# 41 matmuls of ones, read by nobody, put into planned TensorE waits of the first batch

## The chip, the cores and the metric

The kernel runs on one core of one Trainium2 chip. The metric is the device time of one execution in microseconds (us). The three runs shown of the kernel before took 528.59, 529.96 and 799.26 us, with a median of 529.96 us. The profile was taken from one further execution, which took 529.17 us.

## The reference

The input is q, k and v of 8 batches, 8 heads, 576 positions and head size 64, and the weights of a gated feed-forward block. What is computed, for each batch:

```python
# attention: heads 0-3 see the last 32 positions, heads 4-7 every 4th of the last 128
scores = where(mask[h], (q @ k.T) / 8, -1e9)           # 576 x 576 per head
attn   = exp(scores - max) / (sum + 1e-9)
x      = (attn @ v)                                    # heads side by side: 576 x 512
# expert
h      = relu(x @ w_in)                                # 576 x 1024
conv   = conv_w[0]*h[s-1] + conv_w[1]*h[s] + conv_w[2]*h[s+1]
out    = (h * sigmoid(conv)) @ w_out                   # 576 x 512
```

## The kernel before

**Tiling.** Attention is done for pairs of heads: four pairs a batch, two with the plain window (kind 0) and two with the dilated one (kind 1), so 32 pairs in all. Scores are computed in strips of 32 queries by 64 keys, since the mask leaves nothing else: one pair is some 72 to 80 small matmuls at line 298 (64x32 weights, 64 columns moving). For the pairs of `EASED`, a few bf16 matmuls of `ones` with the mask (line 285) open the banks first, the maximum is taken straight from PSUM on VectorE (L311 to L315), and nine small exponentials run on ScalarE (L322). VectorE then normalizes and transposes (L340 to L345), and some 84 to 88 small matmuls at line 356 multiply by v. ScalarE copies the result out as the high part (L408, tiles x0a, x1a and so on), and VectorE forms the low part (L411, x0b, x1b), so that products with float32 accuracy can be made from three passes over fp32r operands.

**Expert.** The first product (line 436, 128x288) and the second one (line 478, 128x512) each take three passes per piece (`TERMS`). ScalarE and VectorE do relu, taps, sigmoid and the split of the gated values.

**Weights.** The 16 weight pieces (8 of w_in, 8 of w_out, and one of conv_w) come in as 64-bit floats. For each, ScalarE (L513, L528) and VectorE (L515 to L522) take the words apart, and for ten of them (`SUMMED`) TensorE adds three products in a bank (lines 531 to 533), from which ScalarE copies the low part out (L536). These pieces are prepared in the first batch, among the attention of the first pairs.

**Banks.** PSUM has eight banks of 128x512 float32, all in one tile `banks`. Banks 0 to 3 (pool `att`) are one slot for a pair's scores or its product with v. Banks 4 and 5 (pool `mm`) and 6 and 7 (pool `nn`) serve the expert's products and the sums of the weights; the first pairs in `EARLY` have their scores there.

**Order.** `Planner` holds every piece of work as a task with an engine, a cost in us, a due time and the tasks that it follows. `Planner.order` (line 145) goes through time by these costs: it gives every task a start, picks by due time among the tasks of an engine that could start within 0.25 us of the earliest one, and holds buffers and banks until their last user has ended. The result is one list sorted by planned start, and the instructions are issued in this list's order. Each engine works through its own instructions in that order; what it really waits for on the chip are semaphores, not the planned times. Loads are issued from SyncE's queue (SP) in the same order: qk at L270, v at L272, weights at L504. A load waits there until the tile that it overwrites has been read.

Of the kernel before, what the change touches and what calls it, by code (L numbers as in the profile page):

```python
# [77 lines left out]
EARLY = (0, 1, 3)  # L78
SUMMED = (0, 3, 4, 5, 6, 7, 8, 11, 12, 14)
LEFT = 16  # L80
NU, NX, NR, NW, NT = 10, 7, 4, 3, 2
ONE = dict(start=True, stop=True, skip_group_check=True)

# [17 lines left out]
class Planner:  # L101
# [43 lines left out]
    def order(self):  # L145
        waiting = {t: len(t.after) for t in self.tasks}
        users = {}
        for t in self.tasks:
            for p in t.after:
                users.setdefault(p, []).append(t)  # L150
        ready, last, mode, done = {}, {}, {}, []
        for t in self.tasks:
            if not waiting[t]:
                ready.setdefault(t.engine, []).append(t)
        while len(done) < len(self.tasks):
            best = None
            for e, ts in ready.items():
                at = [(self.start(t, last.get(e), mode.get(e)), t) for t in ts]
                at = [x for x in at if x[0] is not None]
                if not at:  # L160
                    continue
                first = min(x[0] for x in at)
                s, t = min((x for x in at if x[0] <= first + self.WINDOW), key=lambda x: (x[1].due, x[0]))
                if best is None or first < best[0]:
                    best = (first, s, t)
            _, s, t = best
            for b in t.uses:
                if b.t is None:
                    slot = min(self.free[b.pool])
                    self.free[b.pool].remove(slot)  # L170
                    b.t, b.slot = slot[2], slot
            t.end, last[t.engine] = s + t.cost, t
            if t.table is not None:
                mode[t.engine] = t.table
            for b in t.uses:
                b.left -= 1
                b.end = max(b.end, t.end + self.late(t))
                if not b.left:
                    self.free[b.pool].append((b.end, b.slot[1], b.slot[2]))
            ready[t.engine].remove(t)  # L180
            done.append((s, t))
            for n in users.get(t, ()):
                waiting[n] -= 1
                if not waiting[n]:
                    ready.setdefault(n.engine, []).append(n)
        return [t for _, t in sorted(done, key=lambda x: x[0])]


@with_exitstack
def attn_moe(ctx: ExitStack, tc: tile.TileContext, qk_p, qk_d, v_p, v_d, w_in, w_out, conv, mask, out):  # L190
    nc = tc.nc
# [7 lines left out]
    ones = const.tile([128, 128], BF16, name="ones")  # L199
# [3 lines left out]
    plan = Planner()  # L203
# [23 lines left out]
    banks = psum.tile([128, 8, 512], F32, name="banks")  # L227
# [3 lines left out]
    bank = lambda ps: banks[:, ps.t]  # L231
    chunk = lambda u, n=512: u.t[:, LEFT:LEFT + n]
    body = lambda u: u.t[:, 1:S + 1]
# [313 lines left out]
    made = plan.add("POOL", 0.6, -1e4, lambda: make_identity(nc, ident))  # L547
    made = plan.add("ACT", 0.29, -1e4, lambda: nc.scalar.copy(out=ones, in_=ident), [made])
# [21 lines left out]
    wored = [weights(w_out[c], 512, WO[c], pair=(wo[0][c], wo[1][c]), summed=c + NF in SUMMED) for c in range(NF)]  # L570
    for b in range(B):
        expert(b, [attention(b, p) for p in range(NP)], wired, wored, conved)
    with tc.manual_schedule():
        for t in plan.order():
            t.run()


def _layouts(q, k, v, moe_w_in, moe_conv_w, moe_w_out):
# [84 lines left out]
```

## Time and profile before

| what | value |
|---|---|
| profiled execution | 529.17 us |
| its span, first to last instruction | 527.4 us |
| time around the span | 1.77 us |
| TensorE (PE) matmuls | 505.9 us busy, 7656 matmuls |
| PE weight loads (PEld) | 442.2 us busy |
| VectorE (DVE) | 393.4 us |
| ScalarE (ACT) | 304.9 us |
| mean granted TensorE clock | 0.984 |
| share of PE in the chain of waits | 92% |

The page of the profile divides the span in 40 slices and gives the busy share of each engine and the TensorE clock that was granted. The chain of waits goes back from the last instruction to whatever released each step. The timeline lists instructions in order of time; neighbours of one kind are drawn together, and an idle time ahead of a row stands in brackets with what ended it. "issue" is time in which the engine waited for nothing that the profile shows. Ends of matmuls are modelled, so the time from one row's start to the next row's start is the better measure of what a group of matmuls takes.

### The profile page before, as it was taken

What the parts mean: (1) busy time and instruction counts of PE and PEld (TensorE: products, weight loads), DVE (VectorE), ACT (ScalarE), POOL (GpSimd) and SP (SyncE); (2) the same over time, 40 slices, a digit from 0 to 9 for tenths busy, and PEclk for the clock granted to TensorE, in tenths of its full rate; (3) what the DMA queues carried; (4) which work ended last, traced back from release to release, by engine and by line L of the source; (5) the groups of instructions that cost most, each with busy time, mean ns of one, the idle gap of its engine ahead of it and who ended that gap; (6) DMA issues with size and microseconds to landing.
All of it is one profiled execution on the core that took longest, in us unless ns stands there. A gap on an engine that the chain in (4) does not pass through costs nothing.

```text
span 527.4 us, 17134 instructions
## 1 busy us (share of the span) xinstructions
PE 505.9 (96%) x7656; PEld 442.2 (84%) x7656; DVE 393.4 (75%) x675; ACT 304.9 (58%) x642; POOL 1.4 (0%) x26
## 2 busy tenths in 40 slices
PE   4579999999999999999999999999999999999997
PEld 3457988988877899879988889899889988998885
DVE  5877998999999789968989639997789730872400
ACT  5856887746842267626677337766757631852410
POOL 1000000000000000000000000000000000000000
PEclk9868999999999999999999999999999999999999
DMA  8966654001154541151152224320310011101111
GB/s 300 354 214 225 179 186 170 1 0 62 51 170 156 206 136 36 54 162 52 48 163 95 61 73 150 94 85 21 118 40 21 1 22 41 40 2 41 40 41 60
DMA packets 17274, 52.33 MB, mean 99 GB/s; under 512 B 2096, under 2 KB 2480, under 8 KB 17200
## 3 DMA queue, kind: packets, MB, share of 16 engines
q1 hardware_dynamic: 17200, 51.23, 29.3%
q8 instruction: 60, 0.98, 0.8%
q14 instruction: 14, 0.11, 0.1%
HBM read 41.79 MB, written 9.44 MB: 97 GB/s over the span
## 4 chain that ended last, share of the span: by engine, by line
PE 92%; DMA 3%; ACT 2%; issue 1%; DVE 1%; SPq 0%; ACTq 0%
PE banks L436 40%; PE banks L478 38%; PE banks L356 7%; PE banks L298 6%; PE banks L531 2%; ACT s L322 1%; DMA raw<-in_w_out_dram 1%; DMA qk<-in_qk_d_dram 1%; PE banks L533 0%; PE banks L532 0%; PE banks L285 0%; DVE x2b L411 0%; SPq L504 0%; SPq L270 0%; DVE w L517 0%
## 5 line engine op out<-in xcount | busy, mean ns | idle before, releaser
L448 DVE SCALAR_TENSOR_TENSOR u<-u,conv_sb,u 128x576 f32<-128x576 f32 x128 | 103.5, 816 | 12.9 <-ACT u L454 11.4
L443 ACT ACTIVATE u<-banks 128x288 f32<-128x288 f32 x128 | 51.4, 410 | 52.0 <-PE banks L436 50.6
L489 ACT COPY u<-banks 128x512 f32<-128x512 f32 (+1 forms) x37 | 21.1, 572 | 77.3 <-PE banks L478 76.2
L461 DVE TENSOR_TENSOR u<-u,u 128x576 f32<-128x576 f32 x64 | 47.9, 757 | 11.0 <-ACT u L459 9.9
L459 ACT ACTIVATE u<-u 128x576 f32<-128x576 f32 x64 | 42.9, 683 | 18.4 <-DVE u L448 17.8
L454 ACT ACTIVATE u<-u,conv_sb 128x576 f32<-128x576 f32 x64 | 49.8, 779 | 1.6
L356 PEld LDWEIGHTS banks<-pt,v 32*64 32x64 f32 x2752 | 36.4, 137 | 16.7 <-issue 7.3
L356 PE MATMUL banks<-pt,v 32*64 32x64 f32 (+2 forms) x2752 | 40.5, 233 | 7.2 <-ACT s L322 3.9
L436 PE MATMUL banks<-x2a,wi 128*128 128x288 f32 x160 | 46.0, 302 | 0.0
L436 PE MATMUL banks<-x3a,wi 128*128 128x288 f32 x160 | 45.7, 302 | 0.0
L436 PE MATMUL banks<-x0a,wi 128*128 128x288 f32 x160 | 45.4, 301 | 0.0
L436 PE MATMUL banks<-x1a,wi 128*128 128x288 f32 x160 | 45.2, 298 | 0.0
L298 PE MATMUL banks<-qk 64*32 64x64 f32 x2432 | 35.7, 232 | 9.7 <-DMA qk<-in_qk_p_dram 6.9
L436 PE MATMUL banks<-x4a,wi 128*128 128x288 f32 x160 | 45.0, 296 | 0.0
L298 PEld LDWEIGHTS banks<-qk 64*32 64x32 f32 x2432 | 29.8, 109 | 16.7 <-DMA qk<-in_qk_p_dram 6.9
L436 PE MATMUL banks<-x5a,wi 128*128 128x288 f32 x128 | 36.2, 299 | 0.0
L436 PEld LDWEIGHTS banks<-x2a,wi 128*128 128x128 f32 x160 | 30.3, 189 | 1.5 <-ACT u L443 0.5
L436 PEld LDWEIGHTS banks<-x3a,wi 128*128 128x128 f32 x160 | 29.9, 188 | 1.0 <-ACT u L443 0.2
L436 PEld LDWEIGHTS banks<-x0a,wi 128*128 128x128 f32 x160 | 29.9, 188 | 0.8
L436 PEld LDWEIGHTS banks<-x1a,wi 128*128 128x128 f32 x160 | 30.0, 188 | 0.4
L436 PEld LDWEIGHTS banks<-x4a,wi 128*128 128x128 f32 x160 | 30.0, 188 | 0.2
L478 PE MATMUL banks<-wo,g1a 128*128 128x512 f32 x72 | 28.7, 398 | 0.0
(136 smaller groups left out, 1271.8 us busy)
## 6 DMA issues: line engine op xcount, KB each, us to landing
qk<-in_qk_d_dram SPq DMA_DIRECT2D x16, 672.0 KB, 4.6
qk<-in_qk_p_dram SPq DMA_DIRECT2D x16, 592.0 KB, 4.0
out_dram<-u SPq DMA_DIRECT2D x31, 256.0 KB, 2.0
v<-in_v_p_dram SPq DMA_DIRECT2D x16, 384.0 KB, 3.5
v<-in_v_d_dram SPq DMA_DIRECT2D x16, 384.0 KB, 3.7
raw<-in_w_out_dram SPq DMA_DIRECT2D x8, 512.0 KB, 3.7
raw<-in_w_in_dram SPq DMA_DIRECT2D x8, 512.0 KB, 5.1
out_dram<-u SPq DMA_DIRECT2D x10, 128.0 KB, 2.3
```

The lines of the kernel that those rows point to most:

```text
L298: nc.tensor.matmul(banks[quad * 32:quad * 32 + 32, at[bank], c * W:c * W + W], q, k, start=i == 0 and not eased, stop=i == len(parts) - 1, ...
L322: nc.scalar.activation(out=s.t[:, i, :], in_=banks[:, at[bank], c * W:c * W + W], func=AF.Exp, scale=SCALE, bias=m.t[:, i:i + 1], accum_ou ...
L356: nc.tensor.matmul(banks[hd * 64:hd * 64 + 64, bank, o:o + n], v.t[quad * 32:quad * 32 + 32, block // 2, block % 2 * 64:block % 2 * 64 + 6 ...
L436: nc.tensor.matmul(bank(ps)[:, 0:HALF], wi[jw][fc][:, k * 128:k * 128 + 128], x[k].t[jx][:, hf * HALF:hf * HALF + HALF], start=(k == 0 and ...
L443: relu.append(plan.add("ACT", 0.4, due + 1.6 * u + relued, lambda fc=fc, hf=hf, ps=ps: nc.scalar.activation(out=h[fc].t[:, 1 + hf * HALF:1 ...
L448: nc.vector.scalar_tensor_tensor(out=body(c[fc]), in0=h[fc].t[:, k:S + k], scalar=conv_sb[:, k, fc:fc + 1], in1=body(c[fc]), op0=ALU.mult, ...
L454: t = plan.add("ACT", 0.777, d, lambda fc=fc: nc.scalar.activation(out=body(c[fc]), in_=body(h[fc]), func=AF.Copy, scale=conv_sb[:, 1, fc: ...
L459: t = plan.add("ACT", 0.686, d + shaped, lambda fc=fc: nc.scalar.activation(out=body(c[fc]), in_=body(c[fc]), func=AF.Sigmoid), [t], [c[fc ...
L461: t = plan.add("DVE", 0.755, d + times, lambda fc=fc: nc.vector.tensor_tensor(out=body(c[fc]), in0=body(c[fc]), in1=body(h[fc]), op=ALU.mu ...
L478: nc.tensor.matmul(bank(ps), g[k].t[jg][:, col:col + 128], wo[jw][k], start=(k == 0 and i == 0), stop=(k == NF - 1 and i == 2))
L489: t = plan.add("ACT", 0.16 + 0.00093 * (c1 - c0), out_due + by_block * u + copied, lambda ps=ps, o=o, c0=c0, c1=c1: nc.scalar.copy(out=chu ...
L531: nc.tensor.matmul(bank(ps), ident, words(t), start=True, stop=False)
```

## The change

`order` now also keeps each task's planned start (`start_at`) and returns the planned starts with the tasks. A new function `filled` walks through TensorE's tasks up to a planned start of 60 us (`FILLED`). Where the plan has a gap between the end of one task and the start of the next, it looks for a bank of the pools `mm` and `nn` that no task holds over the whole gap, and puts as many fill matmuls there as the gap holds, by 0.43 us each in the first gap and 0.23 us each in the later ones, rounded down. A fill multiplies the 128x128 bf16 tile `ones` with 512 columns made of the same tile, into the free bank. Nothing reads what it writes. The fills stand in TensorE's instruction order just ahead of the task whose planned start ends the gap. Due times, costs and the order of all other tasks are as they were. A fill that writes a bank which another engine has read also waits for that reading to have ended.

Going through the plan's costs gives these 41 fills:

| planned gap (us in the plan) | fills | bank | task that follows | that task's first row in the timeline before |
|---|---|---|---|---|
| 2.84 to 6.90 | 9 | 7 | scores, first pair | 6.91 |
| 7.61 to 8.66 | 4 | 7 | scores, second | 8.21 |
| 10.42 to 10.66 | 1 | 7 | weight sum | 10.62 |
| 16.94 to 17.42 | 2 | 7 | scores, fourth | 16.91 |
| 19.03 to 21.58 | 11 | 6 | product with v, first | 20.95 |
| 22.53 to 24.17 | 7 | 6 | scores, fifth | 23.91 |
| 25.78 to 26.02 | 1 | 7 | weight sum | 27.96 |
| 28.49 to 28.73 | 1 | 7 | weight sum | 32.62 |
| 34.71 to 34.95 | 1 | 7 | weight sum | 39.63 |
| 37.68 to 37.92 | 1 | 7 | first product, L436 | 44.09 |
| 41.27 to 41.51 | 1 | 7 | first product, L436 | 47.34 |
| 47.18 to 47.42 | 1 | 6 | weight sum | 53.17 |
| 52.67 to 52.91 | 1 | 6 | first product, L436 | 58.82 |

The planned gaps ahead of the second and third product with v (30.16 to 31.04 and 31.85 to 33.90, rows 35.48 and 38.58) get none, because every bank of the two pools is held there.

```diff
+FILLED = 60.0
...
-            t.end, last[t.engine] = s + t.cost, t
+            t.start_at, t.end, last[t.engine] = s, s + t.cost, t
...
-        return [t for _, t in sorted(done, key=lambda x: x[0])]
+        return sorted(done, key=lambda x: x[0])
+
+    def filled(self, done, fill, first, until, pools, step):
+
+        held = {}
+        for _, t in done:
+            for b in t.uses:
+                if b.pool in pools:
+                    h = held.setdefault(b, [b.t, t.start_at, t.end])
+                    h[2] = max(h[2], t.end + self.late(t))
+        at, more = first.end + self.late(first), []
+        first = at
+        for s, t in done:
+            if t.engine != "PE" or s > until:
+                continue
+            free = [i for p in pools for _, i in pools[p] if all(h[0] != i or h[2] <= at or h[1] >= s for h in held.values())]
+            for k in range(int((s - at) / step[at == first]) if free else 0):
+                more.append((at + 0.001 * k, lambda i=free[-1]: fill(i)))
+            at = t.end
+        return [run for _, run in sorted([(s, t.run) for s, t in done] + more, key=lambda x: x[0])]
...
+    def fill(i):
+        nc.tensor.matmul(banks[:, i], ones, ones.unsqueeze(1).to_broadcast([128, 4, 128]), start=True, stop=True)
+
+    spots = {p: [(0, i) for i in n] for p, n in (("mm", (4, 5)), ("nn", (6, 7)))}
     with tc.manual_schedule():
-        for t in plan.order():
-            t.run()
+        for run in plan.filled(plan.order(), fill, made, FILLED, spots, (0.23, 0.43)):
+            run()
```

## The prediction

> **What bounds the kernel now.** I read the page first, then the granted clock by stage, then TensorE's timeline, then who releases its waits.
>
> ```profile
> span 527.4 us, 17134 instructions
> PE 505.9 (96%) x7656; PEld 442.2 (84%) x7656; DVE 393.4 (75%) x675; ACT 304.9 (58%) x642; POOL 1.4 (0%) x26
> ```
>
> TensorE is busy in all but 21.5 us of the span, so the bulk of the kernel can't be touched by 41 matmuls. All that can move is in the first 45 us. Busy time by stage, cut where the granted clock changes (columns: stretch and length, PE, PEld, DVE, ACT, POOL, granted clock, DMA share, GB/s):
>
> ```profile
> 16.10:19.50 3.40, 2.14 (x80) 1.33 (x78) 2.57 (x7) 1.03 (x2) 0.00 (x0) 1.00 0.89 324
> 19.50:22.90 3.40, 0.80 (x46) 0.67 (x50) 2.78 (x9) 3.40 (x24) 0.00 (x0) 1.00 1.02 407
> 22.90:26.30 3.40, 2.62 (x118) 2.09 (x114) 3.18 (x7) 3.40 (x19) 0.00 (x0) 0.50 0.95 330
> 26.30:29.70 3.40, 2.42 (x35) 1.12 (x18) 3.31 (x7) 1.03 (x2) 0.00 (x0) 0.50 0.74 250
> 29.70:33.20 3.50, 3.50 (x92) 2.58 (x91) 2.06 (x6) 1.62 (x4) 0.00 (x0) 0.50 0.90 303
> 33.20:36.60 3.40, 3.40 (x82) 1.80 (x83) 2.98 (x8) 2.89 (x19) 0.00 (x0) 0.50 0.42 124
> 36.60:40.00 3.40, 1.74 (x116) 1.51 (x104) 2.20 (x5) 2.54 (x6) 0.00 (x0) 1.00 0.57 204
> 40.00:43.40 3.40, 3.40 (x42) 2.09 (x43) 2.94 (x6) 1.55 (x4) 0.00 (x0) 0.50 0.56 187
> ```
>
> The clock changes in steps of 3.4 us. It fell to half after a step with 0.80 us of TensorE work (19.5 to 22.9), stayed there for four steps, came back at 36.6 after two steps without a pause, fell once more after a step with 1.74 us (36.6 to 40.0), and came back at 43.4. So 17 us ran at half clock. A step with 2.14 us of work (16.1 to 19.5) did not make it fall. TensorE's waits there:
>
> ```profile
> 6.91 1.36 PE L298 MATMUL banks<-qk 64*32 64x64 f32 x72 [6.91 <-DMA qk<-in_qk_p_dram]
> ...
> 17.27 0.97 PE L298 MATMUL banks<-qk 64*32 64x64 f32 x72
> 20.95 0.33 PE L356 MATMUL banks<-pt,v 32*64 32x64 f32 x4 [2.71 <-ACT s L322]
> 22.43 1.55 PE L356 MATMUL banks<-pt,v 32*64 32x64 f32 x84 [1.15 <-ACT s L322]
> ...
> 25.08 0.42 PE L285 MATMUL banks<-kinds_sb,ones 128*128 128x256 bf16 x2 [0.78 <-ACT s L322]
> ...
> 27.55 0.48 PE L298 MATMUL banks<-qk 64*32 64x64 f32 x13 [0.98 <-issue]
> ```
>
> The same 72 score matmuls took 1.36 us at 6.91 and 0.97 at 17.27, so the start of the kernel was slow too. The waits at 20.95, 22.43 and 25.08 are for the exponentials on ScalarE, which reads the banks that TensorE wants. ScalarE in turn waited for a load, as the chain of waits has it (start, us, what):
>
> ```profile
> 11.56 7.47 DMA raw<-in_w_out_dram
> 19.04 0.02 issue
> 19.06 0.66 ACT w L513
> ```
>
> Up to 25.08 the bound is thus the load that lands at 19.03 and ScalarE behind it (3.40 us busy of 3.40 in both stages from 19.5). From 25.08 to 36.9 it is TensorE at half clock.
>
> **What half clock costs.** Sums of weights (E, lines 531 to 533), products with v (V, line 356) and first products (line 436), at half and at full clock, from start to start:
>
> ```profile
> 27.96 2.08 PE L531 MATMUL banks<-w,ident 128*128 128x512 f32 x2
> ...
> 30.82 1.87 PE L356 MATMUL banks<-pt,v 32*64 32x64 f32 x88
> 32.62 2.08 PE L531 MATMUL banks<-w,ident 128*128 128x512 f32 x2
> ...
> 35.48 1.44 PE L356 MATMUL banks<-pt,v 32*64 32x32 f32 x84
> 38.58 1.12 PE L356 MATMUL banks<-pt,v 32*64 32x32 f32 x84 [1.66 <-DVE x2b L411]
> 39.63 1.76 PE L531 MATMUL banks<-w,ident 128*128 128x512 f32 x2
> ...
> 44.09 0.40 PE L436 MATMUL banks<-x2a,wi 128*128 128x288 f32 x1
> ...
> 53.17 1.12 PE L531 MATMUL banks<-w,ident 128*128 128x512 f32 x2
> ...
> 54.60 0.29 PE L436 MATMUL banks<-x1a,wi 128*128 128x288 f32 x1
> ...
> 55.01 0.29 PE L436 MATMUL banks<-x0a,wi 128*128 128x288 f32 x1
> ...
> 57.50 1.40 PE L356 MATMUL banks<-pt,v 32*64 32x64 f32 x88
> 58.82 0.40 PE L436 MATMUL banks<-x2a,wi 128*128 128x288 f32 x1
> ```
>
> An E takes 2.86 us at half clock (27.96 to 30.82, and 32.62 to 35.48) and 1.43 at full (53.17 to 54.60). A V of 88 takes 1.80 against 1.32; one of 84 takes 1.44 (row 35.48) against 1.05 (38.58 to 39.63). The stretch 39.63 to 44.09, an E, three first products and a V of 84, takes 4.46; at full clock 1.43 + 0.41 + 1.05 = 2.89, so 1.57 less.
>
> **The change, part by part.** A fill is nearest to a second product, which also moves 512 columns; at half clock to a pass of an E:
>
> ```profile
> 35.12 0.43 PE banks L533
> ...
> 87.45 0.69 PE banks L478 x3
> ```
>
> So 0.23 us a fill at full clock and 0.43 at half.
>
> *Nine, four, one and two fills (ahead of rows 6.91, 8.21, 10.62, 16.91).* The nine take 3.9 us at half clock and lie in TensorE's 6.91 us of waiting for the first qk; cost nothing. The four take 0.9 to 1.7 us between the first and the second scores, the other three 0.7 to 1.3. They can make these scores late by up to 1.7 us, and with them SP's loads that overwrite qk. I take nothing, because all that follows waits for the load landing at 19.03 with the DMA engines 0.89 to 1.02 busy; without that cover it would be +1.7. On the other side the clock may come up before 9 us, worth 1.36 - 0.97 = 0.4 at each score group, equally hidden.
>
> *Eleven fills (ahead of 20.95).* 11 x 0.23 = 2.5 us inside the 2.71 of idle time. Cost nothing; if they start late, TensorE still has 1.15 us of waiting at 22.43. Their use is the clock: the stage 19.5 to 22.9 goes from 0.80 us of work to about 2.0 (0.80 and what of the fills lies behind 19.5). That is near the 2.14 that held and above the 1.74 that did not. I take it that it holds.
>
> *Seven fills (ahead of 23.91).* With full clock the V at 22.43 ends 22.43 + 1.12 = 23.55, seven fills end at 25.16, and scores, openings included (0.42), start at 25.6 and end at 26.6, or at 27.5 if the 0.98 of issue stays, against 27.96.
>
> *The chain after that.* The next waits come from these rows of DVE and ACT:
>
> ```profile
> 29.16 0.69 DVE L522 SCALAR_TENSOR_TENSOR r<-raw,w 128x512 fp32r<-128x512 uint32 x1
> ...
> 32.10 0.43 DVE L515 TENSOR_SCALAR w<-w 128x512 int32<-128x512 int32 x1 [1.44 <-ACT w L513]
> ...
> 33.46 0.82 DVE L411 TENSOR_TENSOR x1b<-banks,x1a 128x512 fp32r<-128x512 f32 x2 [0.20 <-ACT x1a L408]
> ...
> 37.70 0.82 DVE L411 TENSOR_TENSOR x2b<-banks,x2a 128x320 fp32r<-128x320 f32 x2 [1.16 <-ACT x2a L408]
> ...
> 32.73 0.70 ACT L408 CAST x1a<-banks 128x64 fp32r<-128x64 f32 x2 [0.65 <-PE banks L356]
> ...
> 36.97 0.70 ACT L408 CAST x2a<-banks 128x256 fp32r<-128x256 f32 x2 [0.88 <-PE banks L356]
> ```
>
> First E and V: 26.6 to 27.5, plus 1.43 + 1.32 and two single fills, gives 29.8 to 30.7. The second E needs r, done at 29.85, and ends at 31.3 to 32.2 (before: 35.48). The V behind it needs the bank that x1b reads until 34.28. That moves only by DVE's 1.44 of waiting, which ends with TensorE's first E: to 32.84, so this V gains 35.48 - 32.84 = 2.6. The next V waits for x2a and x2b. On ACT, x2a stands behind nine exponentials, which wait for the same piece of DVE's work and move with its 1.44; x2a had then waited 0.88 more for TensorE, and that goes: 1.44 + 0.88 = 2.3. ACT's 0.65 ahead of x1a can go too, if the first V is early enough for it: 2.9. I take the middle, 2.6. VectorE thus keeps what TensorE alone would have saved beyond it: twice 1.43, 0.48 and 0.39 are 3.7, and the issue wait.
>
> *The stretch from 39.63* gains 1.57 with full clock. The two Vs ahead of it keep waits of over a microsecond between them and get no fills, as now, when the clock fell in that step. Between 0 and 1.57 I take 0.3.
>
> *Seven single fills.* Two are in the sum above. The other five stand where TensorE has no wait (39.63, 44.09, 47.34, 53.17, 58.82) and each delays all behind it: 5 x 0.23 = 1.15; 1.35 if one runs at half clock, 0 if the change of shape there hides it. I take 1.15.
>
> Behind that TensorE no longer waits:
>
> ```profile
> 43.40:46.80 3.40, 3.40 (x135) 2.50 (x126) 1.82 (x4) 1.85 (x4) 0.00 (x0) 1.00 0.41 139
> ```
>
> From here a shift of its work goes to the end, as PE carries the chain. **Sum:** 2.6 + 0.3 - 1.15 = 1.75 us less: 529.17 - 1.75 = 527.4 us. The profiled execution lies 0.8 below the median of the runs shown (529.96); I allow that much either way.
>
> **Rivals.** *The clock stays full throughout* (chance 0.2). For it: idle times after the change are short. Against it: 36.6 to 40.0, where 1.74 us of work were not enough, and no fills come there. The time: 2.9 + 1.57 - 1.15 = 3.3 less, 525.9. [...]
>
> *No gain* (0.15). The clock falls a step later, or VectorE, over 9 tenths busy from 22.9 to 29.7, keeps all but about 1.15 us, which the five single fills use up: 529.2.
>
> *Slower* (0.12): the eleven don't hold the clock, since most of them lie ahead of 19.5 or the steps lie otherwise, and the seven run at half clock in front of the scores. They end at 22.43 + 1.55 + 3.01 = 27.0 instead of 25.08: +1.9, all of it on TensorE's chain up to 36.9. Two single fills at 0.43 and the other five for 1.35 make 4.1: 533.3. It decides at whether the first E still takes 2.86. If the seven bring the clock back by the next step, this rival is gone, since then an E saves 1.43 again.
>
> *Instruction supply.* The issue wait of 0.98 us in the scores at 27.55 shows that TensorE's stream can stop for itself. 41 matmuls and their weight loads shift where such stops fall, all through the kernel. I have no reason for a sign: 1 us either way, in the range and in no chance; 0.03 is left for what I don't see.
>
> **How the numbers follow.** My forecast has 0.5 and lies from 526.4 to 528.4. With the full clock (0.2; its lower end 2.9 + 1.57 - 0.2 = 4.3 less, 524.9) and no gain (0.15; upper end 529.2 + 0.8 and half of the 1 us above) the range is 524.9 to 530.5. A difference of 2%, about what a measurement of this kernel can tell from no change, is 10.6 us. All half-clock time together is worth 17 / 2 = 8.5, less than that, and the slower rival is at 0.8%. Faster by over 2%: 0.01, slower by over 2%: 0.02, within: 0.97.
>
> **What would show it.** Right: granted clock 1.00 from 22.9 on in the changed trace, E from 27 at 1.43 us each, V's wait for x2b longer than 1.66, VectorE's wait of 1.44 for L513 gone, single fills with no wait ahead of them, everything from 45 us on about 1.8 us earlier. The step on the second fall: half clock for one step near 37 to 40. Wrong: an E of 2.86 behind the fills, scores later than 25.44, a fill waiting for ACT, or new issue waits of a microsecond.

## The result, and the profile after

The changed kernel took 524.73 us in the median (523.14 to 526.7) against 529.94 for the kernel before: a ratio of 0.9904 with a 95% interval from 0.9874 to 0.9933. Three later comparisons of the same kernel on other occasions gave 0.993, 0.994 and 0.9926 (below), so the gain is 3.3 to 5.2 us. The forecast was 527.4 with a range from 524.9 to 530.5: right in direction, too small in size. The three later times, 524.98, 525.73 and 525.44 us, lie inside that range; the first lies just below it. Its profiled execution took 524.88 us.

The page of the changed kernel, first lines:

```profile
span 523.1 us, 17214 instructions
PE 509.4 (97%) x7697; PEld 443.1 (85%) x7697; DVE 392.7 (75%) x675; ACT 304.5 (58%) x642; POOL 1.4 (0%) x26
```

Busy time by stage in the changed kernel (columns as in the prediction):

```profile
16.80:20.20 3.40, 3.40 (x88) 1.92 (x86) 2.27 (x7) 2.10 (x11) 0.00 (x0) 1.00 1.01 394
20.20:23.60 3.40, 2.44 (x94) 1.67 (x93) 3.06 (x10) 3.40 (x25) 0.00 (x0) 1.00 1.01 398
23.60:27.00 3.40, 3.40 (x86) 2.10 (x83) 3.15 (x8) 2.41 (x10) 0.00 (x0) 1.00 0.93 311
27.00:30.40 3.40, 2.55 (x94) 1.84 (x92) 3.37 (x9) 2.43 (x6) 0.00 (x0) 1.00 0.65 215
30.40:33.80 3.40, 1.96 (x87) 1.19 (x85) 3.33 (x9) 3.40 (x21) 0.00 (x0) 1.00 0.70 264
33.80:37.20 3.40, 2.66 (x86) 2.11 (x87) 2.76 (x6) 2.11 (x5) 0.00 (x0) 0.51 0.82 282
37.20:40.60 3.40, 3.40 (x56) 2.28 (x55) 2.25 (x5) 1.10 (x2) 0.00 (x0) 0.50 0.35 112
```

The clock stayed full from 16.8 to 33.8 and then fell for two steps of 3.4 us, after a step with 1.96 us of TensorE work. That is one execution: in the three later profiles of the same kernel the clock fell near 16 for one step, and again near 36 to 37 for one or two. TensorE's timeline in the changed kernel (start, length; L596 are the fills, L319 scores, L552 weight sums, L377 products with v, L457 first products):

```profile
17.95 2.55 PE L596 MATMUL banks<-ones 128*128 128x512 bf16 x11
20.43 0.33 PE L377 MATMUL banks<-pt,v 32*64 32x64 f32 x4
...
22.84 1.68 PE L596 MATMUL banks<-ones 128*128 128x512 bf16 x7
...
24.70 1.00 PE L319 MATMUL banks<-qk 64*32 64x64 f32 x72
...
25.86 1.02 PE L552 MATMUL banks<-w,ident 128*128 128x512 f32 x2
...
29.18 0.42 PE L377 MATMUL banks<-pt,v 32*64 32x16 f32 x12 [0.85 <-issue]
...
29.76 1.02 PE L552 MATMUL banks<-w,ident 128*128 128x512 f32 x2
...
31.68 1.11 PE L377 MATMUL banks<-pt,v 32*64 32x32 f32 x84 [0.43 <-DVE x1b L432]
34.54 1.59 PE L377 MATMUL banks<-pt,v 32*64 32x32 f32 x84 [1.75 <-DVE x2b L432]
...
36.47 1.91 PE L552 MATMUL banks<-w,ident 128*128 128x512 f32 x2
...
41.24 0.48 PE L457 MATMUL banks<-x2a,wi 128*128 128x288 f32 x1
...
55.98 0.49 PE L457 MATMUL banks<-x2a,wi 128*128 128x288 f32 x1
```

Set against the rows of before, the first weight sum is 2.10 us earlier (27.96 to 25.86), the third product with v 4.04 (38.58 to 34.54), and the row of 58.82 is 2.84 earlier. The span is 4.3 shorter. So some 1.5 us were won behind 56 us, where the change added nothing. That shows in TensorE's waits behind 62 us, all of kind "issue" (total us, times, longest), first before, with the longest of them as a row of the timeline, then after:

```profile
PE banks L356 <- issue: 1.7, 2, 1.1
PE banks L298 <- issue: 0.8, 1, 0.8
```

```profile
86.52 0.33 PE L356 MATMUL banks<-pt,v 32*64 32x32 f32 x12 [1.11 <-issue]
```

```profile
PE banks L377 <- issue: 1.2, 1, 1.2
```

The three waits before stand in the chain of waits, at 85.42, 184.03 and 236.41 us (1.11, 0.60 and 0.79 us), and so does the one of 1.24 us after, at 81.97.

### The profile page after: what moved, and what is told of

Same layout as the page of the kernel before. It is cut to its first block, busy times and chain, and to the rows that moved or that the text cites. A ratio compares the mean times of both kernels' runs of the same rounds, so it can differ in the third digit from the quotient of the medians.

```text
span 523.1 us, 17214 instructions
## 1 busy us (share of the span) xinstructions
PE 509.4 (97%) x7697; PEld 443.1 (85%) x7697; DVE 392.7 (75%) x675; ACT 304.5 (58%) x642; POOL 1.4 (0%) x26
## 4 chain that ended last, share of the span: by engine, by line
PE 94%; DMA 3%; ACT 1%; issue 1%; SPq 0%; DVE 0%; ACTq 0%
PE banks L457 40%; PE banks L499 38%; PE banks L377 7%; PE banks L319 6%; PE banks L552 1%; DMA raw<-in_w_out_dram 1%; DMA qk<-in_qk_d_dram 1%; ACT s L343 1%; PE banks L596 1%; PE banks L554 0%; PE banks L553 0%; PE banks L306 0%; SPq L293 0%; DVE x2b L432 0%; SPq L525 0%
## 5 line engine op out<-in xcount | busy, mean ns | idle before, releaser
L469 DVE SCALAR_TENSOR_TENSOR u<-u,conv_sb,u 128x576 f32<-128x576 f32 x128 | 103.5, 817 | 12.7 <-ACT u L475 11.1
L377 PEld LDWEIGHTS banks<-pt,v 32*64 32x64 f32 x2752 | 35.6, 134 | 14.4 <-issue 7.8
L457 PE MATMUL banks<-x2a,wi 128*128 128x288 f32 x160 | 46.1, 303 | 0.0
L457 PE MATMUL banks<-x3a,wi 128*128 128x288 f32 x160 | 45.7, 302 | 0.0
L457 PE MATMUL banks<-x0a,wi 128*128 128x288 f32 x160 | 45.4, 300 | 0.0
L457 PE MATMUL banks<-x1a,wi 128*128 128x288 f32 x160 | 45.3, 298 | 0.0
L457 PE MATMUL banks<-x4a,wi 128*128 128x288 f32 x160 | 45.2, 297 | 0.0
L377 PE MATMUL banks<-pt,v 32*64 32x64 f32 (+2 forms) x2752 | 39.7, 230 | 5.2 <-issue 2.1
L319 PEld LDWEIGHTS banks<-qk 64*32 64x32 f32 x2432 | 28.7, 106 | 9.7 <-issue 4.0
L319 PE MATMUL banks<-qk 64*32 64x64 f32 x2432 | 34.2, 224 | 2.3 <-DMA qk<-in_qk_d_dram 2.1
L457 PE MATMUL banks<-x5a,wi 128*128 128x288 f32 x128 | 36.2, 299 | 0.0
L457 PEld LDWEIGHTS banks<-x2a,wi 128*128 128x128 f32 x160 | 30.3, 190 | 1.4 <-ACT u L464 0.5
L457 PEld LDWEIGHTS banks<-x3a,wi 128*128 128x128 f32 x160 | 30.0, 188 | 1.0 <-ACT u L464 0.2
L457 PEld LDWEIGHTS banks<-x0a,wi 128*128 128x128 f32 x160 | 29.9, 188 | 0.8
L457 PEld LDWEIGHTS banks<-x1a,wi 128*128 128x128 f32 x160 | 30.0, 188 | 0.4
L457 PEld LDWEIGHTS banks<-x4a,wi 128*128 128x128 f32 x160 | 30.0, 188 | 0.1
```

The lines of the kernel that those rows point to most:

```text
L319: nc.tensor.matmul(banks[quad * 32:quad * 32 + 32, at[bank], c * W:c * W + W], q, k, start=i == 0 and not eased, stop=i == len(parts) - 1, ...
L377: nc.tensor.matmul(banks[hd * 64:hd * 64 + 64, bank, o:o + n], v.t[quad * 32:quad * 32 + 32, block // 2, block % 2 * 64:block % 2 * 64 + 6 ...
L457: nc.tensor.matmul(bank(ps)[:, 0:HALF], wi[jw][fc][:, k * 128:k * 128 + 128], x[k].t[jx][:, hf * HALF:hf * HALF + HALF], start=(k == 0 and ...
L469: nc.vector.scalar_tensor_tensor(out=body(c[fc]), in0=h[fc].t[:, k:S + k], scalar=conv_sb[:, k, fc:fc + 1], in1=body(c[fc]), op0=ALU.mult, ...
```

## The experiments

Two theories stood against each other. A: the gain is the clock. B: TensorE's instruction stream is loaded in pieces (before, the page has 60 packets on the queue q8, "instruction", for 15,312 matmuls and weight loads, some 255 each); the 82 added instructions (41 matmuls with their weight loads) shift where it is cut, and so where TensorE waits for its own instructions. The times are medians, with the kernel before run beside them on the same chip. The diffs are shortened, and the comments in them were added here.

**Small fills at the same places.** The same 41, with 1 column in place of 512:

```diff
-        nc.tensor.matmul(banks[:, i], ones, ones.unsqueeze(1).to_broadcast([128, 4, 128]), start=True, stop=True)
+        nc.tensor.matmul(banks[:, i, 0:1], ones, ones[:, 0:1], start=True, stop=True)
```

> The same 41 matmuls at the same places, but with 1 column moving in place of 512, so that TensorE's instruction stream is as long as in the changed kernel and the waits stay idle. Theory A (the gain is the clock): half clock comes back as before, some 17 us of it between 20 and 45, the first weight sum (L531 of before, near 27) takes 2.86 us, and the row that stood at 58.82 before stays within 1 us of it; time within 1.5 us of before. Theory B (a good part of the gain is a shifted instruction supply): the issue waits change as in the changed kernel (0.98 in the scores gone, one of 1.2 instead of three for 2.5 us behind 62), and 1.3 to 2.3 us of the 5 us are kept with the clock still falling.

This gave 524.82 us against 528.74, ratio 0.9931 (0.99 to 0.9961): most of the gain is there without TensorE being kept busy. In this kernel's stages the clock fell at 23.2 as before, but came back two steps earlier:

```profile
19.80:23.20 3.40, 1.02 (x71) 0.88 (x72) 2.99 (x9) 3.40 (x26) 0.00 (x0) 1.00 1.01 399
23.20:26.60 3.40, 2.68 (x121) 2.07 (x110) 3.18 (x7) 3.40 (x18) 0.00 (x0) 0.50 0.90 320
26.60:30.00 3.40, 3.40 (x36) 1.55 (x33) 3.33 (x9) 0.80 (x2) 0.00 (x0) 0.50 0.92 324
30.00:33.40 3.40, 3.02 (x124) 2.07 (x126) 2.85 (x7) 3.31 (x15) 0.00 (x0) 0.99 0.75 236
```

Its timeline has no issue wait in the fifth scores, and behind 62 us its issue waits are one of 0.2. The load that landed at 19.03 before landed at 19.12 here, and the third product with v still started 2.46 us earlier than before (36.12 instead of 38.58):

```profile
25.52 1.56 PE L319 MATMUL banks<-qk 64*32 64x64 f32 x72
...
27.06 2.06 PE L552 MATMUL banks<-w,ident 128*128 128x512 f32 x2
...
36.12 1.32 PE L377 MATMUL banks<-pt,v 32*64 32x32 f32 x84 [1.87 <-DVE x2b L432]
```

```profile
PE banks L377 <- issue: 0.2, 1, 0.2
```

**The shift by itself.** Small matmuls only in TensorE's first wait, 41, 64 or 128 of them, and the changed kernel for comparison:

```diff
+        more = [(first + 0.001 * k, lambda: fill(7)) for k in range(41)]      # or 64, 128; no others, 1 column each
```

> The changed kernel itself once more, as the corner of a square of four: fills of 512 columns and 82 instructions more. Both theories: about 0.990 of before. It is there so that the other three are compared with it on the same chip.

> No fills; 41 matmuls of 1 column in TensorE's first wait, ahead of the first scores, where it idles for 4 us: the instruction stream is moved by 82 instructions and nothing else. Theory A (clock): as before, ratio 0.998 to 1.002. Theory B (the instruction stream comes in pieces of 256 instructions, 60 packets of 16 KB for some 15,300 instructions, and where a piece ends decides how long TensorE waits for the next): as the 41 small fills, near 0.993, with the issue wait in the scores at 27 gone and at most 1.2 us of issue waits behind 62 us.

> The same with 128 matmuls of 1 column, so 256 instructions: the pieces end at the same work as in the kernel before. Theory B: the gain of the 41 is gone, ratio 0.998 to 1.002, issue waits again in the scores near 27 and of some 2.5 us behind 62. If it stays near 0.993, it isn't where the pieces end, but something else that the small matmuls bring.

> 64 matmuls of 1 column in the first wait, half a piece of the instruction stream. If where the pieces end is what decides, the issue waits come at the same counts of matmuls from the start as in all other traces (350, 477, 605 and so on, steps of 128), whatever stands there, and so in other places of the work than with 0, 41 or 128; the ratio can lie anywhere from 0.993 to 1.003. If waits come at the same places of the work as in one of those, the pieces are not the cause.

The changed kernel gave a ratio of 0.993 (0.9903 to 0.9957); 41 in front 0.995 (0.9932 to 0.9968); 64 in front 0.9962 (0.9939 to 0.9985); 128 in front 1.0022 (1.0 to 1.0043). With 256 instructions more the gain is gone, and the wait in the fifth scores stands at the same place of the work as before, behind 59 of 72 matmuls (shift of 128):

```profile
26.91 1.13 PE L322 MATMUL banks<-qk 64*32 64x64 f32 x59
28.89 0.47 PE L322 MATMUL banks<-qk 64*32 64x64 f32 x13 [0.85 <-issue]
```

How many matmuls had started when a wait of this kind ended is in the PE column of a stretch from 0 to that time. Before, up to the wait in the fifth scores:

```profile
0.00:27.50 27.50, 14.00 (x477) 9.71 (x478) 19.75 (x49) 18.43 (x75) 1.37 (x26) 0.92 0.90 328
```

With the shift of 128, and with that of 41 (two waits):

```profile
0.00:28.80 28.80, 17.50 (x605) 13.05 (x606) 19.70 (x48) 18.37 (x75) 1.37 (x26) 0.93 0.87 311
```

```profile
0.00:20.00 20.00, 9.95 (x350) 7.32 (x350) 12.63 (x31) 11.12 (x35) 1.37 (x26) 1.00 0.86 301
0.00:31.90 31.90, 18.11 (x605) 12.70 (x605) 23.16 (x56) 20.23 (x78) 1.37 (x26) 0.89 0.89 314
```

In the changed kernel, up to the wait at 29.18:

```profile
0.00:29.10 29.10, 22.87 (x605) 13.33 (x605) 21.94 (x54) 20.01 (x78) 1.37 (x26) 1.00 0.92 342
```

350, 477, 605: steps of 127 or 128 matmuls, with their weight loads some 255 instructions. Where there is such a wait, it stands at one of these counts, whatever work is there. With 64 in front the counts 350 and 477 fall in the fourth scores, behind 32, and one matmul ahead of the end of the first product with v:

```profile
17.66 0.45 PE L322 MATMUL banks<-qk 64*32 64x64 f32 x32
19.84 0.66 PE L322 MATMUL banks<-qk 64*32 64x64 f32 x40 [1.72 <-issue]
...
23.64 1.70 PE L380 MATMUL banks<-pt,v 32*64 32x64 f32 x83 [1.15 <-ACT s L346]
26.60 0.21 PE L380 MATMUL banks<-pt,v 32*64 32x32 f32 x1 [1.26 <-issue]
```

The trace also has the times of the instruction queue's packets (q8 on the page: 60 packets, 0.98 MB, so 16 KB each). Each of these waits ended 1.2 to 1.6 us after one of them:

```
kernel      matmuls before the wait   packet            TensorE goes on   later by
before      477                       25.05 to 26.05    27.55             1.51
before      1751                      84.18 to 85.12    86.52             1.40
before      3281                      182.03 to 183.35  184.63            1.29
before      4173                      235.01 to 235.97  237.20            1.23
after       605                       26.48 to 27.58    29.18             1.60
after       1752                      80.88 to 81.82    83.21             1.38
shift 128   350                       14.44 to 15.33    16.94             1.61
shift 128   605                       26.37 to 27.47    28.89             1.43
shift 128   1879                      83.98 to 84.91    86.37             1.46
shift 128   4301                      236.12 to 237.07  238.39            1.32
```

1751 and 1879, 4173 and 4301 lie 128 apart, as a shift by one piece demands. The steps of some 255 instructions agree with the 15,312 over 60 packets.

The other traces bear this out. In the 20 traces together TensorE's timelines have 80 issue waits of 0.1 us or more. Each stands within 4 matmuls of a count of 222 + 127.45 k, and the packet that ended last ahead of it is in every case packet k of its trace, counted from 0; TensorE went on 1.21 to 1.61 us after its end. The places are thus fixed by the program. The lengths are not: with 41 more matmuls the issue waits behind 62 us come to 0.2 and 0.8 us in the two profiles with small fills, to 0.7 to 1.2 in the four of the changed kernel, and to 1.7 with all 41 in front.

**Full fills at a shift of 128.** The four large gaps in finer pieces, 36, 16, 40 and 26 matmuls of 128 columns:

```diff
+            n = {9: 36, 4: 16, 11: 40, 7: 26}.get(n, n)
+            few = n < 3        # 512 columns as before; the others 128
```

> The fills at their places and about as long as in the changed kernel, but cut into 36, 16, 40 and 26 matmuls of 128 columns in the four large gaps, 128 matmuls in all, so 256 instructions: clock as in the changed kernel, pieces ending as before. Theory A: ratio 0.990. Theory B alone: 1.000. Both add: about 0.996, half clock for 7 us or less, and issue waits of some 2.5 us behind 62.

This gave 529.19 against 528.78, ratio 0.9993 (0.9969 to 1.0017). That is 1.05 us below the 128 small ones (530.24), which is less than these runs can tell from nothing. There was half as much time at half clock (mean granted clock 0.993 against 0.985), and no gain over before: nearest to Theory B alone. The count of 477 falls in the first product with v here, behind 56 of its 88 matmuls, and the wait there was 2.34 us:

```profile
22.28 0.79 PE L380 MATMUL banks<-pt,v 32*64 32x64 f32 x52 [0.16 <-ACT s L346]
25.41 0.58 PE L380 MATMUL banks<-pt,v 32*64 32x32 f32 x32 [2.34 <-issue]
```

**Which fills.** Parts of the change alone (the others left out):

```diff
+            n = n if 19.0 < at < 23.0 else 0      # late18: the eleven and the seven
+            n = n if n > 1 else 0                 # nosingle34: no gap of one fill
```

> Only the eleven and the seven fills (planned gaps 19.03 and 22.53). Theory A: the clock holds from 22.9 to about 34, and the row of 58.82 comes at 55.5 to 56.5: the five single fills (1.15) are gone, and the 0.7 that the changed kernel had won before 20 us may be lost. A rival: without the first sixteen, the start runs at half clock until 12.7 as before, the steps lie otherwise, and the clock falls near 23 all the same: no gain, or a loss of up to 2 us from fills at 0.43.

> Without the eight gaps of one fill each (one ahead of the first weight sum, seven from planned 25.8 on): 9, 4, 2, 11 and 7 are left. If a single fill costs its 0.23, the row of 58.82 comes about 1.2 us earlier than in the changed kernel (55.98), at 54.8, and the time is some 1.2 less than the changed kernel's. If they cost nothing (hidden in the change of shape) it stays at 56.0. If they do hold the clock, half clock lasts longer than the 6.8 us of the changed kernel.

> As nosingle34, and also 6 and 15 fills of 256 columns in the two planned gaps where every bank is held (ahead of the second and third product with v, rows 31.68 and 34.54 of the changed kernel), written without a start flag to the upper half of bank 4, which nobody reads. Theory A: the second fall of the clock (33.9 in the changed kernel) does not come, weight sum and products from 36.5 to 41.2 take 1.5 us less, and the time is 1.5 to 2.5 below nosingle34, about 521.5. Rival: the products with v wait for VectorE and start no earlier, the fills delay them by up to 0.5 us each, and nothing is gained over nosingle34.

*late18*: 526.8 against 528.74, ratio 0.9961 (0.9931 to 0.9991). The clock held from 13.5 to 37.4, so in this execution the front fills weren't needed for that, and the fifth scores had an issue wait of 0.96 again: with 18 ahead, the count of 477 falls in them, behind 41 of their 72 matmuls. *nosingle34*: 524.18, ratio 0.9908 (0.9877 to 0.994). (It has 33 fills, as the single one ahead of the first weight sum went too.) *held* (fills of 256 columns also ahead of the second and third product with v, in columns that nobody reads): 525.45, ratio 0.9937 (0.9914 to 0.9959), against what I expected. Its mean granted clock was the highest of these, 0.996, and its time 4 us above the 521.5 that I had put down; it also has another shift, 54, and its fills hold back the second product with v, as the first of them wait for an exponential themselves (0.46 us), and I can't tell the two apart.

With the stream of 41 kept, 512 columns in some fills and 1 in the rest:

```diff
+            whole = n > 2 or n == 2 or at < 11.0    # large512; n == 11: eleven512; n == 7: seven512
```

> All 41 matmuls in place, so the instruction stream is the changed kernel's, but the seven single ones from the planned gap at 25.8 on have 1 column. If a full single fill costs its 0.23 us, the row of 58.82 comes some 1.2 us earlier than in the changed kernel (55.98 there) and the ratio is about 0.991, better than the changed kernel's on the same chip (0.993); if the singles cost nothing, 0.993. This is also the version that could beat both.

> The stream of 41 again, with 512 columns in the eleven fills of the planned gap 19.03 alone, 1 column in the other thirty. If those eleven alone keep the clock, it holds past 23 (it fell at 23.2 with 41 of 1 column) and the first weight sum takes 1.43 us; the time is then within 1 us of the 41 small ones (ratio 0.993), since the two kernels with full and with small fills were. If the eleven need the work ahead of them or the seven behind, the clock falls near 23 all the same.

> The same with 512 columns in the seven fills of the planned gap 22.53 alone. The slower rival of the prediction, by itself: the clock falls near 23, the seven run at 0.43 and end near 27, and the fifth scores start some 1.5 to 2 us later than with small fills (25.52). If the seven then bring the clock back a step earlier, the weight sum behind them takes 1.43 and little is lost by 45 us; if not, the row of 58.82 comes 2 us later than with small fills, ratio 0.997.

The ratios are 0.9922 (0.9892 to 0.9953), 0.994 (0.9916 to 0.9964) and 0.9933 (0.991 to 0.9955). The eleven alone did not hold the clock: the first weight sum took 2.84 us (26.62 to 29.46). With the seven alone the slower rival of the prediction comes about:

```profile
24.51 3.17 PE L599 MATMUL banks<-ones 128*128 128x512 bf16 x7
...
28.08 1.37 PE L321 MATMUL banks<-qk 64*32 64x64 f32 x72
...
29.42 1.10 PE L554 MATMUL banks<-w,ident 128*128 128x512 f32 x2
```

Each took about 0.43, and the scores started 2.56 later than with small fills (25.52). But the clock came back at 29.4, the weight sum behind took 1.50 (29.42 to the next product at 30.92), it didn't fall again, and the time is that of small fills: paid and refunded, as the rival's last sentence had it.

**Full against small on one chip.**

> The changed kernel again. If the clock is worth what the prediction said (2.6 + 0.3 - 1.15 = 1.75 us), it is 1.5 to 2 us faster than tiny41b on the same chip. If the fills give back what the clock saves, the two agree within 0.7 us, with a ratio near 0.992.

> The same stream with 1 column in every fill: ratio near 0.993 whatever the clock is worth; the difference to same41b is the worth of the clock less the length of the fills.

> Fills of 512 columns in the large gaps alone (9, 4, 2, 11, 7): ratio near 0.991. Without the single ones the clock's worth is not given back there: if it is 2 us or more, this beats tiny33 by that.

> The same 33 places with 1 column. If the gain is the shift alone, near nosingle34b (within 0.7 us); if the full clock is worth 2 us where no single fills stand, 2 us slower than it, ratio near 0.995.

Against 528.98 before: changed kernel 525.73 (0.994, 0.9918 to 0.9962), 41 small ones 525.46 (0.9936, 0.9914 to 0.9958), 33 full ones without single fills 524.12 (0.9917, 0.9886 to 0.9947), 33 small ones 526.28 (0.9948, 0.9925 to 0.9971). In the changed kernel, full fills gain nothing over small ones that these runs can tell (0.3 us slower, about 0.8 either way); without the single fills they gain 2.2 us, about 1 either way.

> The changed kernel's instruction stream with 1 column in the seven late single fills. Against same41c on the same chip it has the price of full single fills alone. If each costs 0.23 - 0.045 more than a small one on the path, it is 0.9 to 1.3 us faster than same41c; if the change of shape hides half of them, as the rows around 50.5 in the changed kernel's timeline look (a fill of 0.23 ahead, and the weight sum behind it 0.12 shorter), 0.3 to 0.6 us.

> The changed kernel, for comparison with large512b: ratio 0.990 to 0.994.

The full stream with small late single fills: 524.0 (0.991, 0.9875 to 0.9944); the changed kernel: 525.44 (0.9926, 0.9901 to 0.995), against 529.08. The seven late single fills cost 1.4 us together, known to about 1.3 us either way.

So, at the change's own shift: 3.5 us from the shift (528.98 to 525.46, 41 small at its places; 2.6 with all 41 in front), 1.4 to 2.2 from the clock (0.9936 with small fills less 0.991 with full ones and small single ones, of 529, from two occasions; 2.2 at a shift of 33), and 1.4 given back by single fills. The version without them (nosingle34, 0.9908 and 0.9917) beats the kernel before, and on one chip the changed kernel's median by 1.6 us.

## Why the prediction was wrong

Taken step by step:

- *Bound up to 25.08: the load and ScalarE.* Right. TensorE still waited 0.96 us for the exponentials at 21.73. The load landed at 18.33 instead of 19.03, which moved all behind it by 0.7; the first load landed anywhere from 6.3 to 8.0 in these traces, so I don't count that as the change's.
- *Nine, four, one and two fills at no cost.* Right: the nine ended at 6.33, just as the first scores began, and the second scores began at 8.85 (9.08 before). The clock did come up early, at 6.6; in the chain of waits the second scores took 1.13 us instead of 1.61, and the single fill behind them took back 0.34.
- *The eleven hold the clock.* The clock held, but in part by luck of where the steps lie. The eleven ran from 17.95 to 20.43, nearly all of it in the step from 16.8 to 20.2, and not in the one that had 0.80 us of work before. The 2.44 us of the step from 20.2 to 23.6 are the end of the eleven (0.31 us), products with v and, from 22.84 on, 0.76 us of the seven. With the seven at one column (eleven512) the step behind the eleven, from 20.5 to 23.9, had 1.76 us and the clock fell.
- *The seven, and the scores at 25.6.* They came at 24.70, of which 0.7 is the load.
- *The chain after that, 2.6.* The third product with v gained 4.04: 0.7 from the load, the 2.6, and 0.7 more that I had left to VectorE. The bound was the right one, as the waits of 0.43 and 1.75 for x1b and x2b show. The cause was not: with 41 small fills, and the load landing as before, the same row gained 2.46. In these traces, then, at most 0.9 us of the 4.04 is left for fills that keep TensorE busy.
- *Second fall, 0.3.* It fell, as the row of 1.74 had said, but for two steps and not one. From the third product with v to the row of 41.24 it took 6.70 us (34.54 to 41.24) against 5.51 before, so this was a loss of 1.2, not a gain; 0.40 of it is the single fill at 36.07.
- *Single fills, 1.15.* 1.4 measured, for all seven and against ones of one column.
- *Sum of these, 1.75.* Full against small fills in the changed kernel: nothing that the comparison can tell (525.73 and 525.46).
- *Instruction supply: "I have no reason for a sign: 1 us either way, in the range and in no chance."* This is the step that failed. It is worth 3.5 us at a shift of 41, more than the rest together, and it is why 524.73 lies below the range. What I had called a scatter is in its places fixed by the program: the waits come at counted places. The kernel before had issue waits of 0.98 and 2.5 us on TensorE's path, which a shift could take away. I had read over the 2.5: "All that can move is in the first 45 us" and "Behind that TensorE no longer waits" are wrong, as the row at 86.52 and those at 184.63 and 237.20 show. Whether a shift can also add time is at the edge of what the runs tell: at 128 it was 1.5 us longer, ratio 1.0 to 1.0043. One of the prediction's signs of being wrong, a new issue wait of a microsecond, did appear: 1.24 us ahead of 83.21.

How the shift gains is partly shown. Behind 62 us issue waits go from 2.5 to 0.2 and 0.8 in the two traces with 41 small fills, and to 1.7 with all 41 in front. Ahead of it the 0.98 in the scores goes, and in these traces the clock comes back at 30 to 31 instead of 36.6 to 38.6 where that wait stood (before, and shift of 128). Each of these is one execution; over all executions the mean clock hardly differs (0.985 before, 0.986 to 0.9875 with 41 small ones), so how much of the 3.5 us goes through the clock stays open.

An estimate for it: with a half-clock time of 2 x (1 - clock) x span, an execution spends on average 15.6 us at half clock before, 14.0 with 41 small fills. Over 297 executions of the 14 programs measured, 1 us more at half clock went with 0.33 us more time among executions of one program. By that the 1.6 us less is worth some 0.5 of the 3.5. It is a relation between executions and not an experiment, and it gives too much rather than too little for the fills: for full ones with small late single ones (4.9 us at half clock) it gives 3.0 us over small ones, where 1.4 was measured.

The rivals: the clock did not stay full throughout in any of the four profiles; the mean granted clock was 1.0 in 4 of the changed kernel's 36 executions. The slower rival did not come. Where its start did, in seven512, the clock was back at 29.4, about when the first weight sum began (29.42); with small fills it was back at 30.0, so that the seven brought it back is not shown. "No gain" was the right answer for the changed kernel's fills as fills, and the wrong one for the kernel.

## What to carry to other kernels

Adding TensorE instructions was two changes here: what they do (1.4 to 2.2 us won by the clock, 1.4 lost to single fills), and a shift of all later ones against the counts, 127 or 128 matmuls apart, at which issue waits came (3.5 us with 41 small matmuls at the same places). Control such a change with an equally long stream of one-column matmuls, and look in the trace for issue waits at a fixed count of matmuls. The shift saved more here than the 1.75 us that the change was meant to bring, and a comparison that doesn't control for it can put this down to the wrong cause. The 33 fills in the gaps that hold more than one won 2.2 us against small ones; the seven single ones that stood mostly where TensorE had no wait cost 1.4 us together, about what they take (7 x 0.23 = 1.6).

## What the runs showed of the hardware

- The profile draws the clock as 1.00 from 0 to the first recorded change, at 12.7 us before. The 72 scores took 1.36 us at 6.91 and 0.97 at 17.27, and the first two matmuls of a weight sum 2.07 us at 10.62, as at 27.96 (2.08, drawn clock 0.50), against 1.12 at 53.17: it was half there.
- The clock fell after steps of 3.4 us with 0.80 and 1.74 us of TensorE work (before), 1.02 (tiny41) and 1.96 (after), and held after 2.14 (before), 2.44 and 2.55 (after): a step that was busy for 1.96 us of 3.4 was followed by a fall. Busy time alone does not decide it: a step with 1.89 us (10.0 to 13.4 in the changed kernel) and one with 1.73 (13.4 to 16.8 with 41 in front) held too. Coming back took between one and four steps, one of them busy throughout (29.7 to 33.2 before) and still not enough; why is open.
- TensorE went on 1.2 to 1.6 us after the end of the packet whose number goes with the count of matmuls (that this packet brings the instructions is concluded from the matching numbers); the waits this left were up to 2.34 us each in the rows shown (block128), mostly among the small matmuls of scores and products with v.
